# First layer-norm tiles through a ScalarE square root, normalising allowed on Pool, and a new queue order

## Chip, cores and metric

One core of one Trainium2 chip. The metric is device time in microseconds (us) of one execution, as the median of several runs. Profiles are of one execution each; times inside them count from the start of its span. Pool is GpSimd.

## The reference

A pre-layer-norm attention (16 heads, 8 positions at a dilation of 2) and an MLP with two more layer norms, on 2048 rows of 448 values in bf16. Cut to what matters here, the layer norms:

```python
def _layernorm(x, axis=-1, eps=1e-5):
    m = jnp.mean(x, axis=axis, keepdims=True)
    v = jnp.var(x, axis=axis, keepdims=True)
    return (x - m) / jnp.sqrt(v + eps)

x = A_x
h  = x + attention(_layernorm(x), A_wqkv, A_wo)
# B(y): y1 = y + gelu(_layernorm(y) @ w1) shifted @ w2 ; y1 + gelu(_layernorm(y1) @ w3) @ w4
h2 = h + B(_layernorm(h), B_w1, B_w2, B_w3, B_w4)
```

## The kernel before

The 2048 rows are four chunks of four tiles (128 rows each). Every layer norm of a tile is: statistics on VectorE (`bn_stats`, `bn_aggr`), inverse deviation and negative mean times it on Pool (`inv_std`), and one *normalising* of 512 or 448 elements per partition, then a transpose, on TensorE or by a transposing DMA issued from SyncE's queue. There are 64 normalisings. Tags: `A1` is the layer norm before the projections (V, QK), `B1` the one before `W1`, `X` the one kept for the residual, `L3` the one before `W3`.

```python
def inv_std(slot, kind, i0, n, s1=1.0, s2=EPS, with_nmr=True):
    pool("tensor_scalar", 200, out=vtmp[...], in0=mv[..., 1], scalar1=s1, scalar2=s2, op0=ALU.mult, op1=ALU.add)
    pool("tensor_tensor", 420 + 160 * n, out=rstd[...], in0=vtmp[...], in1=mhalf[:, 0:n], op=ALU.pow)
    ...                                            # nmr = -mean * rstd, for ScalarE's form

def normalize(slot, kind, i, out_ap, in_ap, dve_only=False):
    kv = dict(out=out_ap, in0=in_ap, scalar1=m_, scalar2=r_, op0=ALU.subtract, op1=ALU.mult)
    if dve_only:
        return dve("tensor_scalar", 390, **kv)
    op = S.add_many("flex", ...)                   # the queue order decides the engine
    op.opts = {"dve": [("tensor_scalar", kv)],
               "act": [("activation", dict(out=out_ap, in_=in_ap, func=ACT.Identity, scale=r_, bias=n_))]}
    op.occ = {"dve": 308, "act": 652}; op.lat = {"dve": 390, "act": 745}
    return op

def phase_A1(c):
    for il in range(4):
        ln_stats(0, xin[:, i, :], i)
        if c == 0 and il % 2 == 1:
            inv_std(0, 0, i - 1, 2, with_nmr=False)
    ...
    for il in range(4):
        normalize(0, 0, 4 * c + il, ..., dve_only=c == 0)
        transpose_pe(...) if c in TPE else transpose_dma(...)
```

A table `_ORDER` lists every operation once, by number. It gives each engine its queue (each runs in order), the PSUM banks, and, by a suffix `v`, `a` or `p`, the engine of a flexible operation (VectorE, ScalarE, Pool). Waits are derived from it.

Of the kernel before, what the change touches and what calls it, by code (L numbers as in the profile page):

```python
# [5 lines left out]
ACT = mybir.ActivationFunctionType  # L6
# [222 lines left out]
WARM = 18  # L229
LATE = 2  # L230

START = 158


_ORDER = """
2 1 3 4 7 8 5 6 14 12 13 0 16 15 63 62 71 17:7 76 9 10 127 20 18 21 19 26 24 22 23 27 25 28 29 30 33 34:7 31:6
36 32a 37:5 39 40:4 35v 38v 41v 72 44a 45v 47v 108 46a 11 61 102 66 106 75 105 94 100 101 109 48:60 49 50 82:42
83 84 53a 78 69 42 43a 97 110 85 56 98 129 107 135 104 133 67 131 136 130 132 134 137 138 86a 139 140 51 177 178
179 54v 59 60 87a 52:7 181 175 64 55a 180 95 57 217:24 150v 182 70 73 141v 88:60 89 176 90 91 144v 65 68 218 220
93a 151:3 183 145:2 58 147v 146a 142:5 148:4 92v 184 152v 143v 149v 74 99 198 185 186 193v 221 77 219 231:06 232  # L240
234 163:24 164 153 233 165 167a 222:76 191a 189v 103 235 166 168a 227 113p 194 228 229 114p 118p 112p 115a 117a
111p 116a 119p 196 187a 162 169:20 170 171 172 223 224 225 190 343:64 173a 96 195 174a 200 236:32 226 158:1 241
344 242 237 197 346 202 199 161a 375:2 378a 238 154:64 357:02 358 203 188 243 201 239 244 240 204 230 206 345
192 155 120p 360 205 359 361 156 159a 207 157 160a 212a 347 245:02 246 208a 247 248 249 250 251 253 257 255 254
258 252 256 259 386:46 268 387 388 270 389 214a 390a 261 362:32 391a 363 260 367 210a 368 262 269 122 121 364
271 369 379 265a 380:40 209 365 348:76 349 353 381 382 350 351 354 383 384a 385a 532:26 370 352 371:40 372 373
535 79 533 355 376a 374 216 525:26 377a 266v 211 263v 264v 267 366 81 356 526 215 528 272a 536 413:40 414 415
534 537:6 527 529 213 530:2 417 419 126 421 416 275a 418 420 538a 423 425 422 426 424 427 274v 429 428 430 531a
540 438 539 541 542 432v 273a 433v 431v 434v 276:64 277 278 436 437 279 435 280 401:02 402 403 404 281 288v 286a
292v 290v 289a 283v 287v 285v 282v 293v 291v 284v 392:46 439 406a 441v 405a 543 546 442v 393 394 545 544 395  # L250
397a 398a 400 294:02 295 296 298 297 299 302 300 303 301 306 304 305 307 309v 308v 310 125 440a 128 444:46 445
446 447 407:20 408 409 448 449 451v 460v 410 453v 456v 454a 458a 452a 457a 455v 461a 450v 459v 663:64 412a 411v
666 664 547 550 549 548 462:20 463 464 465 466 467 470 396:5 468 474 469 472 473 471 475 399a 313:26 314 315
551:04 316 80 317 552 553 555 554 556 557 559 561 558 562 123 478 476 477 479 124 563 564 560 480v 565 482v 483v
318 481a 486 574 667 567 319:62 320 321 322 324 325:04 326 327 328 566 568 323 331:62 311 312 572v 332 333 334
484 329 330 569v 571v 570v 576 665 335 573 336 670:04 337:7 443a 671 340:6 575 673 674 338 672 341 668:4 577
675:0 676v 487 580a 578a 489:62 669a 490 491 581v 485 493 678 677 582:04 583 584 586 585 587 492 679 680 681 683
684 682 488 494 598v 495:06 496 497 498 592v 599v 588v 596v 590v 594v 591v 589a 593a 595v 597v 600:24 601 602
604 603 606 607 605 608 612 610 613 609 611 614 500 615 616 617 499 501:06 502 686 503 688 505 504 507:42 508
509 685 506 511 687 510 619a 621v 339 513:7 618v 579a 626 689:40 690 514 512 620a 691 693 695 692 697 698 694  # L260
696 701 699 702 700 712 519:7 522:6 705 622 624 520 703 704 523 706 707a 521 623 633:04 634 635 636 710v 515
709v 637 708v 711 639:62 640 641 638 643 625 642 627:40 644 628 629 720:26 630 713 631 714 721 722 723 632 725
715 724 718v 645:04 730v 731 736v 732v 738v 729v 740v 737v 733a 734 728v 735a 727a 726v 739 646 647 649 719a 648
516:7 650 716v 342 517 717v 809:02 810 811 813 812 814 817 815 816 746:64 818 819 820 821 822 747 748 749 751
756 757 750 758 524 754 759 657:3 654:5 651:7 755 752 753 760 762 761 763 658 824v 660:6 823v 825 764a 741 742
743 652 659 744:7 655 766v 767v 765a 771 770 745 653 828:42 829 830 768 661 834:60 831 835 836 837 832 833
840:24 841 838 839 842 843 844 785:06 786 845 846:42 847 848 849 851 827 656 826 769 850 772 787 788 790 789
773:42 774 775 776 777 778 779:06 780 518 791:24 792 793 795 794 781 782 783 662 784 852:3 853 796 854 797:7
803:6 798 799 804 805 806:7 807 800:6 808 801 802 855:7 856 857
""".split()  # L270


def _fast_path(nc, es, flag, A_x, A_wqkv, A_wo, B_w1, B_w2, B_w3, B_w4, out):
# [15 lines left out]
    def sb(name, shape, dt):  # L289
        return es.enter_context(nc.sbuf_tensor(name, shape, dt))  # L290
# [38 lines left out]
    nmr = sb("nmr", [128, 4, NTL], F32)  # L329
    vtmp = sb("vtmp", [128, 4, NTL], F32)  # L330
    mhalf = sb("mhalf", [128, 4], F32)
    fint = sb("fint", [128, 32], I32)
    fmax = sb("fmax", [128, 1], F32)
    fbit = sb("fbit", [128, 1], BF16)
# [6 lines left out]
    def tag(name):  # L341
        S.tag = name
# [4 lines left out]
        return S.add_many("pe", calls, cost, cost + 166, mode=mode)  # L347

    def act(out_ap, in_ap, func, n, **kw):
        table = {ACT.Exp: "exp", ACT.Gelu_apprx_tanh: "gelu"}.get(func)  # L350
        lat = 186 + n / 1.2 + 93 * sum(isinstance(v, bass.AP) for v in kw.values())
        return S.add_many("act", [("activation", dict(out=out_ap, in_=in_ap, func=func, **kw))], lat - 93, lat, table=table)

# [3 lines left out]
    def dve(meth, lat, **kw):  # L357
        return S.add_many("dve", [(meth, kw)], lat - 82, lat)
# [103 lines left out]
    for c in range(1, NCH):  # L462
# [5 lines left out]
    S.add("pool", "affine_select", 300, out=ident[:], in_=ident[:], pattern=[[-1, 128]],  # L468
          compare_op=ALU.not_equal, fill=1.0, base=0, channel_multiplier=1)
    dve("memset", 62, ap=mhalf[:], constant=-0.5)  # L470
    dve("memset", 272, ap=wqk_p[:, :, :, 28:32], constant=0.0)
    pool("memset", 100, ap=hT[:, 0, :, :, 8:16], constant=0.0)
    tag("warm")
# [77 lines left out]
    def inv_std(slot, kind, i0, n, s1=1.0, s2=EPS, with_nmr=True):  # L551
        pool("tensor_scalar", 200, out=vtmp[:, slot, i0:i0 + n], in0=mv[:, kind, i0:i0 + n, 1], scalar1=s1,
             scalar2=s2, op0=ALU.mult, op1=ALU.add)
        pool("tensor_tensor", 420 + 160 * n, out=rstd[:, slot, i0:i0 + n], in0=vtmp[:, slot, i0:i0 + n],
             in1=mhalf[:, 0:n], op=ALU.pow)
        if with_nmr:
            pool("tensor_scalar", 230, out=nmr[:, slot, i0:i0 + n], in0=mv[:, kind, i0:i0 + n, 0], scalar1=-1.0,
                 scalar2=None, op0=ALU.mult)
            pool("tensor_tensor", 220, out=nmr[:, slot, i0:i0 + n], in0=nmr[:, slot, i0:i0 + n],
                 in1=rstd[:, slot, i0:i0 + n], op=ALU.mult)  # L560

    def normalize(slot, kind, i, out_ap, in_ap, dve_only=False):
        r_ = rstd[:, slot, i:i + 1]
        n_ = nmr[:, slot, i:i + 1]
        m_ = mv[:, kind, i, 0:1]
        kv = dict(out=out_ap, in0=in_ap, scalar1=m_, scalar2=r_, op0=ALU.subtract, op1=ALU.mult)
        if dve_only:
            return dve("tensor_scalar", 390, **kv)
        op = S.add_many("flex", [("tensor_scalar", dict(kv, x=n_))], 0, 0)
        op.opts = {"dve": [("tensor_scalar", kv)],  # L570
                   "act": [("activation", dict(out=out_ap, in_=in_ap, func=ACT.Identity, scale=r_, bias=n_))]}
        op.occ = {"dve": 308, "act": 652}; op.lat = {"dve": 390, "act": 745}
        return op

    def lslot():
# [35 lines left out]
    def phase_A1(c):  # L611
        tag("A1_%d" % c)
        s = ls = c % 2
        for il in range(4):
            i = 4 * c + il
            ln_stats(0, xin[:, i, :], i)
            if c == 0 and il % 2 == 1:
                inv_std(0, 0, i - 1, 2, with_nmr=False)
        if c > 0:
            inv_std(0, 0, 4 * c, 4)  # L620
        for il in range(4):
            normalize(0, 0, 4 * c + il, lntm[:, ls, il, :, :], windows(xin[:, 4 * c + il, :]), dve_only=c == 0)
            if c in TPE:
                transpose_pe(ls, il, s)
            else:
                transpose_dma("%d_%d" % (c, il), columns(s, il), lntm[:, ls, il, :, :].rearrange("p a k -> p (a k)"), 1)
        if c > 0:
            tag("Vc_%d" % c)
            pool("tensor_copy", 215, out=hT[:, s, :, :, 8:16], in_=hT[:, 1 - s, :, :, 264:272])
# [311 lines left out]
                   op0=ALU.mult)  # L941

    phase_A1(0)
    pad_wqk()
    phase_V(0)
    init1()
# [535 lines left out]
```

## Time and profile before

| | before |
|---|---|
| median of runs (first three) | 193.94 us |
| span of the profiled run | 192.9 us |
| TensorE busy | 183.2 us (95%) |
| VectorE / ScalarE / Pool busy | 129.7 / 108.6 / 44.2 us |
| one normalising on VectorE / ScalarE | 0.41 / 0.81 us |

TensorE is the bound: what isn't its busy time is 9.7 us. Its waits, stages and opening are shown in the prediction.

### The profile page before, as it was taken

How to read it: one execution, taken by the hardware profiler on the slowest of the kernel's cores; microseconds unless marked ns; L12 is line 12 of the kernel's file. 1: busy time of each engine (PE TensorE's matmuls, PEld its weight loads, DVE VectorE, ACT ScalarE, POOL GpSimd, SP SyncE). 2: the span in 40 equal slices, each digit the busy share in tenths (PEclk: the TensorE clock that was granted, in tenths of full speed). 3: DMA queues.
4: the chain of work that ended last, by engine and by line, in shares of the span. 5: the costliest groups of instructions: out<-in, count | busy, mean ns of one | idle time of the engine just before them, and what ended most of it. 6: DMA issues, size and time to landing. Idle time of an engine off the chain costs nothing.

```text
span 192.9 us, 6787 instructions
## 1 busy us (share of the span) xinstructions
PE 183.2 (95%) x3003; PEld 103.4 (54%) x3003; DVE 129.7 (67%) x312; ACT 108.6 (56%) x140; POOL 44.2 (23%) x107
## 2 busy tenths in 40 slices
PE   7899999999988998999989999999999999999994
PEld 2445645545665764567555454444764557554551
DVE  6899999999997966989773596970079871001221
ACT  2367789757997759859587555045670026554000
POOL 2538750407002402032900023070002300000000
PEclk9999999999999999999999999999999999999999
DMA  5997135411099492920552800427000055000111
GB/s 147 337 294 180 45 58 131 141 31 31 3 159 117 107 227 60 262 102 3 109 115 63 192 3 0 109 65 142 0 3 0 0 135 154 3 0 8 46 51 51
DMA packets 32479, 17.77 MB, mean 92 GB/s; under 512 B 22524, under 2 KB 31932, under 8 KB 32444
## 3 DMA queue, kind: packets, MB, share of 16 engines
q1 hardware_dynamic: 32156, 17.05, 37.6%
q8 instruction: 25, 0.41, 0.9%
q10 hardware_dynamic: 288, 0.23, 0.3%
q14 instruction: 10, 0.08, 0.1%
HBM read 10.07 MB, written 1.90 MB: 62 GB/s over the span
## 4 chain that ended last, share of the span: by engine, by line
PE 72%; DVE 16%; ACT 4%; POOL 3%; issue 1%; DMA 1%
PE ps L1390 72%; DVE st L1390 4%; DVE pt L1390 2%; DVE lntm L1390 2%; DMA xin<-in_A_x_dram 1%; POOL rstd L1390 1%; DVE qk L1390 1%; ACT arena L1390 1%; POOL nmr L1390 1%; DVE xb L1390 1%; DVE xin L1390 1%; DVE osb L1390 1%; ACT qk L1390 1%; ACT pt L1390 1%; ACT vt L1390 1%
## 5 line engine op out<-in xcount | busy, mean ns | idle before, releaser
L1390 PE MATMUL ps<-actT,w_s 64*128 64x512 bf16 (+2 forms) x560 | 44.4, 312 | 0.0
L1390 PE MATMUL ps<-w_s,arena 128*128 128x448 bf16 x224 | 43.4, 353 | 0.4 <-ACT arena L1390 0.4
L1390 DVE TENSOR_TENSOR xb<-ps,xb 128x448 bf16<-128x448 f32 (+1 forms) x26 | 18.5, 725 | 33.7 <-PE ps L1390 33.7
L1390 ACT ACTIVATE arena<-ps 128x512 bf16<-128x512 f32 (+2 forms) x40 | 28.9, 766 | 17.4 <-PE ps L1390 17.4
L1390 PEld LDWEIGHTS ps<-actT,w_s 64*128 64x128 bf16 x560 | 25.9, 94 | 17.1 <-issue 0.4
L1390 PEld LDWEIGHTS ps<-w_s,arena 128*128 128x128 bf16 x224 | 21.4, 98 | 21.5 <-issue 1.0
L1390 PE MATMUL ps<-hT,arena 64*128 64x512 bf16 x224 | 25.8, 377 | 0.0
L1390 POOL TENSOR_SCALAR vtmp<-mv 128x4 f32<-128x4 f32 (+1 forms) x18 | 4.6, 256 | 83.6 <-DVE mv L1390 83.0
L1390 POOL TENSOR_TENSOR rstd<-vtmp,mhalf 128x4 f32<-128x4 f32 (+1 forms) x18 | 18.7, 1041 | 0.8
L1390 DVE BATCH_NORM_STATS2 st<-xin 128x6 f32<-128x448 bf16 x32 | 18.3, 610 | 0.9 <-DMA xin<-in_A_x_dram 0.8
L1390 PEld LDWEIGHTS ps<-hT,arena 64*128 64x128 bf16 x224 | 11.9, 94 | 10.7 <-issue 0.4
L1390 ACT ACTIVATE qk<-ps 128x1024 bf16<-128x1024 f32 x14 | 13.8, 1021 | 5.4 <-PE ps L1390 5.2
L1390 ACT ACTIVATE pt<-ps 128x1024 bf16<-128x1024 f32 x16 | 15.5, 1025 | 2.0 <-PE ps L1390 1.9
L1390 PE MATMUL ps<-arena,hT 64*64 64x448 bf16 (+1 forms) x248 | 15.3, 353 | 0.5 <-DVE hT L1390 0.3
L1390 PE MATMUL ps<-actT,w_p 64*128 64x512 bf16 (+1 forms) x140 | 13.2, 334 | 0.6 <-issue 0.6
L1390 PE MATMUL ps<-wo_s,oT 64*128 64x448 bf16 x128 | 13.1, 350 | 0.6 <-ACT vt L1390 0.6
L1390 DVE COPY gC<-gtm 32x256 bf16<-32x256 bf16 (+1 forms) x23 | 5.1, 223 | 12.5 <-ACT gtm L1390 11.9
L1390 ACT ACTIVATE lntm<-xb,nmr,rstd 128x512 bf16<-128x512 bf16 x5 | 3.9, 807 | 14.8 <-POOL nmr L1390 14.8
L1390 ACT ACTIVATE lntm<-xin,nmr,rstd 128x512 bf16<-128x512 bf16 x8 | 6.3, 818 | 8.8 <-POOL nmr L1390 8.8
L1390 PEld LDWEIGHTS ps<-actT,w_p 64*128 64x128 bf16 x140 | 8.3, 94 | 5.2 <-issue 1.0
L1390 DVE TENSOR_SCALAR lntm<-xin,mv,rstd 128x512 bf16<-128x512 bf16 x24 | 9.6, 444 | 2.2 <-POOL nmr L1390 1.4
L1390 DVE TENSOR_TENSOR pt<-pt,msk 128x1024 bf16<-128x1024 bf16 x16 | 10.9, 713 | 0.2 <-ACT pt L1390 0.2
(84 smaller groups left out, 220.8 us busy)
## 6 DMA issues: line engine op xcount, KB each, us to landing
w_s<-in_B_w_dram SPq DMA_DIRECT2D x6, 448.0 KB, 6.0
rzb<-rz_scratch SPq DMA_DIRECT2D x8, 256.0 KB, 4.6
out_dram<-xb SPq DMA_DIRECT2D x16, 112.0 KB, 1.9
xin<-in_A_x_dram SPq DMA_DIRECT2D x3, 448.0 KB, 7.7
arena<-in_A_wqkv_dram SPq DMA_DIRECT2D x2, 448.0 KB, 6.2
w_s<-in_B_w_dram SPq DMA_DIRECT2D x2, 336.0 KB, 7.5
arena<-in_A_wqkv_dram SPq DMA_DIRECT2D x2, 224.0 KB, 4.6
w_s<-in_B_w_dram SPq DMA_DIRECT2D x2, 224.0 KB, 4.6
```

Of the source, the lines that this page charges most:

```text
L1390: inst = getattr(eng, meth)(**kw)
```

## The change

Three intents: shorten the opening by taking the first inverse deviations off Pool; let Pool, 23% busy, take normalisings from VectorE and ScalarE; lay all queues out anew for that.

```diff
+    def inv_std_first(i0):                        # chunk 0, two tiles at a time
+        act(v, m_[:, :, 1], ACT.Sqrt, 2, bias=epsb[:])
+        dve("reciprocal", 160, out=r_, in_=v)
+        dve("scalar_tensor_tensor", 160, out=n_, in0=m_[:, :, 0], scalar=-1.0, in1=r_, op0=ALU.mult, op1=ALU.mult)
...
-                   "act": [("activation", dict(..., func=ACT.Identity, scale=r_, bias=n_))]}
-        op.occ = {"dve": 308, "act": 652}; op.lat = {"dve": 390, "act": 745}
+                   "act": [("activation", dict(..., func=ACT.Identity, scale=r_, bias=n_))],
+                   "pool": [("tensor_scalar", kv)]}
+        op.occ = {"dve": 308, "act": 652, "pool": 730}; op.lat = {"dve": 390, "act": 745, "pool": 750}
...
-                inv_std(0, 0, i - 1, 2, with_nmr=False)
+                inv_std_first(i - 1)
-            normalize(0, 0, 4 * c + il, ..., dve_only=c == 0)
+            normalize(0, 0, 4 * c + il, ...)
...
+    tag("exp")
+    act(expd[:], epsb[:], ACT.Exp, 1)             # dummy exp; stands last in ScalarE's queue
...
-START = 158
+START = 150
-_ORDER = """ 2 1 3 4 7 8 5 6 14 12 13 0 ...        (all of the table replaced)
+_ORDER = """ 3 14 1 2 12 0 15 17 13 4 7 8 ...
```

In the new table 24 normalisings carry `p`, and 49 other operations after the opening (weight copies, V, QK and probability work) change engine too. The change itself puts 730 and 750 ns on a Pool normalising.

## The prediction

> **What bounds the kernel now.** I read the page first, then the waits of TensorE, then the chain that ended last, then busy time by stage, and last the spread of single durations.
>
> ```profile
> span 192.9 us, 6787 instructions
> PE 183.2 (95%) x3003; PEld 103.4 (54%) x3003; DVE 129.7 (67%) x312; ACT 108.6 (56%) x140; POOL 44.2 (23%) x107
> ```
>
> TensorE is busy for 183.2 of 192.9 us, so all idle time of TensorE together is 9.7 us. The waits of TensorE name where it sits:
>
> ```profile
> PE ps L1390 <- DVE oT L1390: 1.4, 1, 1.4
> PE ps L1390 <- DVE qk L1390: 1.1, 1, 1.1
> PE ps L1390 <- issue: 0.9, 2, 0.6
> PE ps L1390 <- DVE lntm L1390: 0.6, 1, 0.6
> ```
>
> The first is the start: TensorE has nothing before 1.35 us. The last matmul ends at 190.05 and the final VectorE add and store take the other 2.9 us. Neither is touched, so what better ordering could win is 9.7 - 1.4 - 2.9 = 5.4 us, or 2.8%, and only if every wait went. That is the cap on a gain. By stage:
>
> ```profile
> core 0: us, PE busy (x) PEld busy (x) DVE busy (x) ACT busy (x) POOL busy (x), PEclk, DMA share, GB/s
> 9.00:32.00 23.00, 22.37 (x600) 12.28 (x600) 22.16 (x49) 18.01 (x24) 12.24 (x32) 1.00 0.57 148
> 32.00:60.00 28.00, 26.50 (x817) 14.87 (x813) 27.13 (x57) 22.39 (x28) 6.30 (x17) 1.00 0.47 74
> 60.00:78.00 18.00, 16.44 (x281) 11.16 (x283) 13.08 (x40) 13.41 (x19) 4.98 (x14) 1.00 0.62 138
> ...
> 98.00:190.00 92.00, 91.63 (x878) 49.59 (x866) 42.26 (x108) 37.96 (x50) 9.24 (x20) 1.00 0.22 54
> ```
>
> To 60 us VectorE is as full as TensorE (22.16 of 23, 27.13 of 28): there the two engines bound the time together. From 98 us on TensorE has 0.4 us of idle in 92: nothing is to be won there. The opening runs through VectorE and Pool:
>
> ```profile
> 3.50 1.16 DVE st L1390 x2
> ...
> 6.22 0.27 POOL vtmp L1390
> 6.49 0.07 issue
> 6.56 0.76 POOL rstd L1390
> 7.32 0.03 issue
> 7.34 0.99 DVE lntm L1390 x2
> 8.33 0.68 DVE hT L1390 x2
> 9.01 0.04 issue
> 9.05 10.23 PE ps L1390 x194
> ```
>
> The first projection matmul can't start before the fourth transposed tile is copied, at 9.05 us. Of that path, the inverse deviation on Pool takes 1.2 us (6.14 to 7.34).
>
> **What the Trainium skill says, and whether the trace agrees.**
> 1. "SBUF — State Buffer", the section on the two separate sides: VectorE and GpSimd share one port pair as an exclusive lock, and the loser blocks for the whole instruction. VectorE needs it in its 2-port modes or with two inputs in SBUF. The trace agrees, and strongly:
>
> ```profile
> L1390 DVE TENSOR_SCALAR lntm<-xin,mv,rstd x24: 379/407/1123, 6.0 to 128.3; 128x512 bf16<-128x512 bf16 x24
> L1390 DVE TENSOR_TENSOR pt<-pt,msk x16: 648/688/1091, 22.6 to 96.8; 128x1024 bf16<-128x1024 bf16 x16
> L1390 POOL TENSOR_SCALAR nmr<-mv x16: 220/227/1789, 15.6 to 152.5; 128x4 f32<-128x4 f32 x14, 128x2 f32<-128x2 f32 x2
> ```
>
> Columns are minimum, median and maximum in ns. The normalising of 1123 ns began at 24.9 us, while Pool was copying w_p from 22.3 to 26.1; the 1789 ns one on Pool, normally 227, began at 90.7, when VectorE ran normalisings and adds back to back.
> 2. "ScalarE: Activation LUTs", What ACT_TABLE_LOAD costs: a load is about 1283 ns. The trace has six at a mean of 1283 ns. The same page's table-set section puts sqrt and exp in different sets.
> 3. "GPSIMD Engine Reference", section 4.1, advises VectorE for elementwise work and says that one-input operations run roughly at line rate on GpSimd. The trace has no normalising on Pool. It has copies: 1072 ns for 512 and 1494 ns for 1024 elements, thus 422 ns per 512 elements, and 256 ns for a tiny TENSOR_SCALAR. My estimate for a normalising of 512 elements is 256 + 422, about 0.7 us, and up to 1.1 us as the copy.
>
> **The change part by part.**
> (a) *The first inverse deviation.* Removed on Pool: two times (0.2 + 0.73) us. Added: two square roots on ScalarE (estimate 0.28 us each from the fixed cost of its small instructions: 0.25 us for 64 elements, plus a pointer operand), two reciprocals and two products on VectorE (0.16 us each, estimate from the 0.17 us of an aggregate and the 0.24 us of a reciprocal of 16). One of four normalisings (0.82 us) goes to ScalarE, which was idle, and ScalarE now copies two of the four transposed tiles. VectorE from 3.50: statistics and aggregates 2.64 (3.50 to 6.14 in the chain, unchanged), + 4 x 0.16, + 3 normalisings at 0.35, + one copy in the shadow and one exposed (0.35 and 0.4), + about 0.1 of waiting for the transpose: 3.50 + 2.64 + 0.64 + 1.05 + 0.75 + 0.1 = 8.7. Before: 9.05. The gain is 0.3 to 0.4, not 1.2 us, because the four small VectorE instructions stand in a queue that was already full. A part of it is that the 0.67 us normalising at 7.34, which ran beside Pool's mask select, is 0.35 again, as Pool's first selects now come later.
> (b) *The tables.* With sqrt first, exp has to be loaded before the first softmax. The dummy exp that should load it early stands last in the queue order, where it costs nothing and does nothing for the softmax. So 1.28 us enters ScalarE's queue between the last V copy and the first exp. Before, that copy ended at 16.6 and exp began at 16.85, on the end of the scores matmul. After, ScalarE also has one more V copy (0.92). I get copy 16.4, load to 17.7, exp at 17.7 instead of 16.85: 0.9 us late. TensorE has other matmuls to run (the second QK group, about 3.2 us), so I put about half, 0.4 us, on its path, before the second scores.
> (c) *Normalising on Pool.* 24 of 64 go to Pool: 16 from VectorE (42 to 26), 8 from ScalarE (22 to 14). In the first 60 us VectorE loses about 5, 5 x 0.4 = 2 us in the stage where it is a bound; ScalarE loses six, but gets weight packing and V copies instead. Against it stands the lock: about 8 Pool normalisings of 0.7 us fall in that stage, and if half of them meet a VectorE instruction that needs the pair and block it for half their length, that is 8 x 0.5 x 0.35 = 1.4 us. Net: 0 to -1 us on VectorE.
> (d) *The order.* Nearly every queue is permuted, with the same 226 matmul groups. Walking the new TensorE queue with durations from the trace, I find scores of the second chunk done about when they were, the second output projection 0.6 us later (VectorE delivers oT and the V copy late), the first W2 level, and the stage before 86 us about 0.5 us ahead. I hold that walk to about 1 us.
>
> Sum: (a) -0.4, (b) +0.4, (c) -0.5, (d) 0 to -0.5; together about -0.5 us on 193.94: **193.4 us**.
>
> **The rivals.**
> *R1: the order pays.* The waits at 48 to 62 us and at 77 us (0.5 + 0.6 + 0.6 + 1.1 us) are all VectorE lateness or issue. If relief of VectorE removes most of them, the gain is 2 to 2.5 us: 191.5. For it: VectorE is the releaser in most of them. Against: the lock hands back part of the relief, and one of them is issue, which no engine causes.
> *R2: the lock takes over.* If Pool normalisings last 1 us and VectorE queues behind most of them, VectorE loses 24 x 0.5 us, of which the 60 to 98 us stage can hide a part; +1.5 to +3 us: 195.5 to 197. For it: the 1123 and 1789 ns cases. Against: from 98 us VectorE is under half busy and its delays vanish.
> *R3: the exp table is exposed whole,* the delay runs through the masks (VectorE) and the first attention: +0.9 instead of +0.4, 193.9.
>
> **Range and chances.** The cap on a gain is 5.4 us and 2% is 3.9 us: a gain of over 2% needs nearly three quarters of all removable waits to go, with no new ones. I give it 0.03. A loss of over 2% needs R2 at its worst: 0.04. Else within 2%: 0.93. The range is my walk's error of 1 us with the two rivals' milder halves: 191.9 to 195.2.
>
> **What would show it.** (a) right if the first projection matmul starts at 8.6 to 8.8 us; wrong if at 9.0 or later. (b) right if a 1.28 us table load stands right before the first exp, which starts at about 17.7, and TensorE has a gap of 0.3 to 0.7 us between 19 and 24 us. (c) right if VectorE's busy time falls by only 4 to 6 us (16 x 0.4, less the stretched ones), Pool's normalisings have a median of 0.7 to 0.8 us and some of over 1 us, and a few VectorE ones pass 0.6 us. (d) right if TensorE's busy time is 183 us within 1 and its idle time 9 to 10 us. The prediction fails if a new wait of over 1 us on a Pool normalising or its transposing transfer stands in TensorE's waits, or if the waits between 48 and 78 us are gone.

## The result, and the profile after

Ratios here and below are the mean time of one kernel's fast runs over that of the other's fast runs of the same rounds, so not quite the ratio of the medians quoted beside them. A run counts as slow when it took over 1.5% more than the fastest of its kernel, else as fast.

| | before | after |
|---|---|---|
| median (lowest to highest) of 4 runs | 194.34 us (193.91 to 195.06) | 207.21 us (206.53 to 207.99) |
| ratio, 95% interval | | 1.066 (1.060 to 1.072) |
| TensorE busy / idle in the span | 183.2 / 9.7 us | 187.6 / 17.2 us |

The changed kernel is 12.9 us slower; the prediction was 193.4. (Granted clock, 0.975 to 0.983 of full speed, is a mean over the run; what lowers it is shown below.) From the head of the changed kernel's page:

```profile
span 204.8 us, 6799 instructions
...
PE 187.6 (92%) x3003; PEld 103.8 (51%) x3003; DVE 126.0 (62%) x299; ACT 108.5 (53%) x141; POOL 89.2 (44%) x125
```

Pool's busy time has doubled, by 45 us, while VectorE was relieved of only 3.7. Single durations of the normalisings of the changed kernel (minimum/median/maximum in ns), first Pool's two tiles, then VectorE's:

```profile
L1403 POOL TENSOR_SCALAR lntm<-xin,mv,rstd x11: 2070/2086/4021, 16.6 to 105.1; 128x512 bf16<-128x512 bf16 x11
L1403 POOL TENSOR_SCALAR xb<-xin,mv,rstd x9: 1862/1868/2017, 68.0 to 161.1; 128x448 bf16<-128x448 bf16 x9
L1403 DVE TENSOR_SCALAR lntm<-xin,mv,rstd x14: 315/407/415, 6.1 to 142.7; 128x512 bf16<-128x512 bf16 x14
```

The same instruction takes five times as long on Pool. The minimum is as long as the median, so this is its own length; only the maxima are stretched by something else. (The last four of the 24, into `lntm` from `xb`, took 2.07 to 3.16 us.) Waits of TensorE in the changed kernel (engine and tile waited for; us in total, times, longest):

```profile
PE ps L1403 <- DMA actT<-lntm: 4.7, 1, 4.7
PE ps L1403 <- ACT osb L1403: 2.5, 1, 2.5
PE ps L1403 <- DVE mv L1403: 2.0, 1, 2.0
PE ps L1403 <- DVE epsb L1403: 1.4, 1, 1.4
PE ps L1403 <- DVE qk L1403: 1.1, 1, 1.1
```

The last two stood in the kernel before too. The first three, 9.2 us, are new. The chains below show Pool behind the first two; for the third it is argued. (`W1` uses `actT`; `osb` is the attention's output before its division, `mv` a tile's mean and variance.) The chain that ended last, for the first (start us, us, what):

```profile
43.49 1.03 POOL rstd L1403
44.52 0.86 POOL nmr L1403 x2
...
45.76 2.09 POOL lntm L1403
...
48.59 1.05 POOL rstd L1403
...
50.46 6.54 POOL lntm L1403 x3
...
58.89 3.71 DMA actT<-lntm
62.60 0.14 issue
```

Before, `W1` of the first chunk began at 58.43 us. Now Pool runs four normalisings of 2.09 us or more between 45.76 and 57.00, the transposing transfer goes out at 58.89, and TensorE starts at 62.74. The same chain at the second wait:

```profile
101.12 6.07 POOL lntm L1403 x2
107.19 1.02 POOL rstd L1403
...
108.51 0.76 ACT xb L1403
109.27 1.83 ACT osb L1403 x2
111.10 0.05 issue
```

The waits name a ScalarE copy to `osb`, but ScalarE had itself waited for Pool's `rstd`, which stood in Pool's queue behind two normalisings of another chunk. One of the two was stretched, beside VectorE's work of the same time:

```profile
101.10 4.02 POOL L1403 TENSOR_SCALAR lntm<-xin,mv,rstd 128x512 bf16<-128x512 bf16 x1
101.27 1.89 DVE L1403 TENSOR_TENSOR pt<-pt,msk 128x1024 bf16<-128x1024 bf16 x3
```

It took 1.9 us longer than its neighbour (2.08 us). That fits the lock which the prediction names, though no run isolates it, and up to 1.9 of the 2.5 us of this wait may be its doing. The third wait ended at 91.54 us. The transfer of its operand went out at 88.73, right after two Pool normalisings (83.49 to 88.71), and took 2.7 us to land, to about 91.4; the VectorE instruction that is named ended at 91.52. Either can have been the last. For Pool speaks that at this place 0.6 us or nothing is left in two kernels below (three on Pool, and short instructions).

Beside the waits, TensorE's clock fell. Busy time by stretch of the changed kernel (after the length of the stretch: TensorE, its weight loads, VectorE, ScalarE, Pool, then PEclk, the granted clock):

```profile
60.50:67.00 6.50, 4.26 (x26) 2.30 (x28) 1.43 (x6) 0.00 (x0) 3.15 (x5) 0.50 0.70 163
67.50:111.50 44.00, 38.23 (x744) 23.97 (x742) 29.90 (x66) 25.52 (x35) 30.60 (x31) 1.00 0.44 109
112.00:115.00 3.00, 3.00 (x22) 1.63 (x20) 1.37 (x4) 2.33 (x3) 0.29 (x1) 0.50 0.10 22
115.50:204.50 89.00, 85.90 (x776) 46.36 (x772) 38.74 (x97) 36.87 (x51) 17.91 (x25) 1.00 0.21 55
```

The clock was 1.00 in these stages before. Here it was halved twice; slices of 0.5 us put the edges at 60.4 and 67.2, and at 111.6 and 115.0 us. TensorE was busy for 4.5 and 3.4 us of that, so by estimate half speed cost 4.0 of its 4.4 us of extra busy time. 7.5 us more idle and 4.4 us more busy make the span's 11.9. The Trainium skill, "TensorE: Matmul & The Clock Gate", Part 1, says that the clock halves after about one idle window of 3.4 us. The half agrees, and the lengths, 6.8 and 3.4 us, are two and one such window. The idle time fits less well: the first drop came 2.4 us into the wait of 4.7, and the second 0.5 us after the end of a wait of only 2.5.

### The profile page after: what moved, and what is told of

It is laid out like the page before. It is cut to its first block, busy times and chain, and to the rows that moved or that the text cites. A ratio compares the mean times of both kernels' runs of the same rounds, so it can differ in the third digit from the quotient of the medians.

```text
span 204.8 us, 6799 instructions
## 1 busy us (share of the span) xinstructions
PE 187.6 (92%) x3003; PEld 103.8 (51%) x3003; DVE 126.0 (62%) x299; ACT 108.5 (53%) x141; POOL 89.2 (44%) x125
## 4 chain that ended last, share of the span: by engine, by line
PE 61%; POOL 15%; DVE 12%; issue 4%; ACT 4%; DMA 2%; SPq 0%; DVEq 0%; POOLq 0%
PE ps L1403 61%; POOL lntm L1403 7%; POOL rstd L1403 3%; DVE st L1403 3%; POOL nmr L1403 2%; DVE xb L1403 2%; DVE xin L1403 2%; DMA actT<-lntm 2%; DVE gC L1403 2%; DVE oT L1403 1%; POOL xb L1403 1%; POOL vtmp L1403 1%; ACT osb L1403 1%; ACT gtm L1403 1%; DVE gB L1403 1%
## 5 line engine op out<-in xcount | busy, mean ns | idle before, releaser
L1403 POOL TENSOR_SCALAR vtmp<-mv 128x4 f32<-128x4 f32 (+1 forms) x16 | 3.9, 243 | 53.4 <-DVE mv L1403 52.7
L1403 POOL TENSOR_SCALAR lntm<-xin,mv,rstd 128x512 bf16<-128x512 bf16 x11 | 25.2, 2298 | 3.0 <-DMA hT<-lntm 2.7
L1403 PE MATMUL ps<-hT,arena 64*128 64x512 bf16 x224 | 26.5, 377 | 0.0
L1403 PE MATMUL ps<-actT,w_p 64*128 64x512 bf16 (+1 forms) x140 | 17.0, 402 | 7.1 <-DMA actT<-lntm 4.7
L1403 POOL TENSOR_SCALAR xb<-xin,mv,rstd 128x448 bf16<-128x448 bf16 x9 | 17.0, 1891 | 0.4
L1403 PEld LDWEIGHTS ps<-actT,w_p 64*128 64x128 bf16 x140 | 9.6, 109 | 13.9 <-issue 7.5
L1403 PEld LDWEIGHTS ps<-hT,arena 64*128 64x128 bf16 x224 | 10.4, 94 | 11.7 <-issue 0.8
L1403 POOL TENSOR_TENSOR rstd<-vtmp,mhalf 128x4 f32<-128x4 f32 (+1 forms) x16 | 16.0, 997 | 0.8
L1403 ACT ACTIVATE qk<-ps 128x1024 bf16<-128x1024 f32 x13 | 12.9, 1023 | 4.4 <-PE ps L1403 4.2
L1403 ACT ACTIVATE lntm<-xb,nmr,rstd 128x512 bf16<-128x512 bf16 x4 | 3.1, 809 | 16.3 <-POOL nmr L1403 16.3
```

What stands on the lines that cost most here:

```text
L1403: inst = getattr(eng, meth)(**kw)
```

## The experiments

Theory P: the loss comes from what a normalising costs on Pool. Theory Q: it comes from the new order, the other engine moves, or the opening. A point is one per cent of the time before.

### All 24 normalisings off Pool

```diff
- ... 151p ... 197p ... 193p ... 216p ... 270p ... 268p 269p ...   (24 entries of the changed order)
+ ... 151v ... 197v ... 193v ... 216a ... 270v ... 268v 269a ...   (engines of the kernel before)
```

> The changed kernel with one thing undone: its 24 normalisings on Pool go back to the engine that the kernel before gave each (15 VectorE, 9 ScalarE); opening, exp table and queue order stay as changed. Theory P (the loss comes from normalisings that last 2.09 us on Pool instead of 0.4 on VectorE or 0.8 on ScalarE): 193.5 to 195.5 us, the 4.7 us wait of TensorE on the transposing transfer gone, TensorE busy time back from 187.6 to 183 to 184 us. Theory Q (the new queue order or the opening with its exp table loses the time): it stays above 203 us with the long waits still there.

Measured: 198.11 us median, ratio 1.018 (1.013 to 1.022). The profile is of the one slow run (200.93), so its waits aren't read. 4.8 of the 6.6 points go with the engine of the normalisings, 9.4 us; 3.4 us stay, more than theory P allowed. (The edit moves 14 to VectorE and 10 to ScalarE; the 15 and 9 in the expectation are a miscount.)

### The same 24 on Pool in the kernel before

```diff
+                   "pool": [("tensor_scalar", kv)]}           (in the kernel before)
- ... 147v ... 193v ... 189v ... 212a ...
+ ... 147p ... 193p ... 189p ... 212p ...                       (the same 24, old numbers)
```

> The kernel before, in its own queue order and with its own opening, with only the same 24 normalisings moved to Pool. Theory P: clearly slower, 199 to 209 us, with new waits of over 1 us on Pool's normalisings or on the transposing transfers behind them, Pool's busy time near 89 us. Theory Q: 193.5 to 196 us, as the engine of the normalisings would not be what costs.

Measured: 207.3 us, 1.067 (1.060 to 1.074). One part of the change alone costs all that the change costs. The long waits of TensorE are only in part the same: 3.3 us on a Pool copy to `qk`, 2.6 us put down to issue, 2.5 us on `osb`; Pool was busy for 95.4 us. The opening and the new order aren't needed for it.

### The opening alone

```diff
  (changed code; the changed order as far as the last transposed copy of chunk 0, then the old order; START = 158)
```

> The kernel before with only the opening of the change: square root on ScalarE, reciprocal and product on VectorE, one of the four normalisings and two transposed copies on ScalarE, the dummy exp last; the rest in the old order with no normalising on Pool. My reading that the opening and the table together cost nothing (the warm-up matmuls, not the deviation, set when the transposes start): 193.9 to 194.9 us, first projection matmul at 8.9 to 9.1 us, table load of 1.28 us before the first exp with no TensorE wait over 0.3 us. The prediction's own sum (opening -0.4, table +0.4) gives the same time, but the first projection matmul at 8.6 to 8.8 us and a wait of 0.3 to 0.7 us near 19 to 24 us. Rival (the exp table is exposed in the first attention): 195 to 196 us.

Measured: 194.44 us, 1.001 (0.996 to 1.006), the first projection matmul at 8.89 us. The table load hides: ScalarE in the changed kernel, around the first exp:

```profile
15.18 1.41 ACT L1403 ACTIVATE vt<-ps 128x896 bf16<-128x896 f32 x2 [0.33 <-PE ps L1403]
16.61 1.28 ACT L1403 ACT_TABLE_LOAD   x1
17.91 1.94 ACT L1403 ACTIVATE pt<-ps 128x1024 bf16<-128x1024 f32 x2
```

It stands where I said and delays exp to 17.91, but TensorE has other matmuls and shows no wait of over 0.2 us there.

### Fewer warm-up matmuls with that opening

```diff
-WARM = 18
+WARM = 15
```

> The kernel before with the opening of the change alone, as e3_opening_alone, and 15 warm-up matmuls instead of 18. There the last of 18 warm-up matmuls ended at 7.44 us, after the first normalised tile was ready at about 6.5, and the first projection matmul came at 8.89. If the warm-up sets when the transposes start, they start by 6.6 to 6.8 us and the first projection matmul is at 8.3 to 8.6 us, with 0 to 0.4 us off the time: 193.8 to 194.4 us (0.998 to 1.001 of before). If it is VectorE's queue that sets it, the first projection matmul stays at 8.8 to 8.9 us and only an idle gap opens ahead of the transposes.

TensorE's opening with 15 (the first line is the warm-up, the second the transposes, the third the projection):

```profile
1.36 5.39 PE L1401 MATMUL ps<-oT 128*128 128x512 bf16 x15 [1.36 <-DVE epsb L1401]
6.59 1.40 PE L1401 MATMUL ps<-ident,lntm 128*128 128x128 bf16 x16
8.44 1.90 PE L1401 MATMUL ps<-arena,hT 64*64 64x448 bf16 x36 [0.45 <-DVE ones L1401]
```

And in the changed kernel, with 18:

```profile
1.35 6.24 PE L1403 MATMUL ps<-oT 128*128 128x512 bf16 x18 [1.35 <-DVE epsb L1403]
7.42 1.06 PE L1403 MATMUL ps<-ident,lntm 128*128 128x128 bf16 x16
9.03 1.29 PE L1403 MATMUL ps<-arena,hT 64*64 64x448 bf16 x21 [0.55 <-DVE hT L1403]
```

So the warm-up held the opening: the first normalised tile is ready at 6.52 us in the changed kernel, but 18 matmuls run to 7.59. Without three of them the projection starts 0.45 us earlier than in the run before. The time, 194.13 us, 0.999 (0.995 to 1.002), doesn't show it: later stages take the gain back.

### What a Pool instruction costs by its form

```diff
+    for _ in range(3):                          # on the kernel before, at the end of Pool's queue
+        pool("tensor_copy", out=Y, in_=X)                                            # 512 elements
+        pool("tensor_scalar", out=Y, in0=X, scalar1=2.0, scalar2=None, op0=ALU.mult)
+        pool("tensor_scalar", out=Y, in0=X, scalar1=2.0, scalar2=0.5, op0=ALU.subtract, op1=ALU.mult)
+        ...  # the same with per-partition values: one; two at 512, 128, 256, 1024 elements
```

> The kernel before with 24 probe instructions put at the end of Pool's queue, after all its own work (about 154 us on), three rounds of eight forms on bf16 tiles of 128 partitions: copy of 512 elements; multiply by one constant, 512; subtract and multiply with two constants, 512; multiply by one per-partition value, 512; subtract and multiply with two per-partition values (the form of the normalising) at 512, 128, 256 and 1024 elements. From the 448 and 512 element normalisings of the changed kernel (1.87 and 2.08 us) the two-value form should be 0.4 us + 3.25 ns per element: 0.82, 1.24, 2.08 and 3.7 us. Theory S (each of the two operations passes costs per element): one-operation forms about 1.1 to 1.3 us, near the copy's 1.07, two-operation forms 2.0 us whether constant or per-partition. Rival T (the per-partition operand is what costs): two constants as fast as one, about 1.1 us, and one per-partition value already near 1.6 us or more. Rival U (the lock against VectorE stretches them): durations scatter, and fall well below 2 us when VectorE is idle.

Pool's timeline in the first of the three rounds, in the order of the edit after the copy (start us, us, form):

```profile
157.38 1.50 POOL L1404 TENSOR_SCALAR lntm<-lntm 128x512 bf16<-128x512 bf16 x1
158.96 1.94 POOL L1404 TENSOR_SCALAR lntm<-lntm 128x512 bf16<-128x512 bf16 x1
161.00 1.56 POOL L1404 TENSOR_SCALAR lntm<-lntm,mhalf 128x512 bf16<-128x512 bf16 x1
162.67 2.08 POOL L1404 TENSOR_SCALAR lntm<-lntm,mhalf 128x512 bf16<-128x512 bf16 x1
164.85 0.79 POOL L1404 TENSOR_SCALAR lntm<-lntm,mhalf 128x128 bf16<-128x128 bf16 x1
165.75 1.22 POOL L1404 TENSOR_SCALAR lntm<-lntm,mhalf 128x256 bf16<-128x256 bf16 x1
167.06 3.78 POOL L1404 TENSOR_SCALAR lntm<-lntm,mhalf 128x1024 bf16<-128x1024 bf16 x1
```

And the copy, all three of them (mean ns last but one):

```profile
L1404 POOL COPY lntm<-lntm 128x512 bf16<-128x512 bf16 x3 | 1.8, 609 | 2.2 <-DMA actT<-lntm 2.1
```

One constant 1.50, two constants 1.94, one per-partition value 1.56, two 2.08, a copy 0.61 us. The three rounds agree (copies 609 to 610 ns, the 1024-element form 3778 to 3779) while VectorE worked beside them for 7.5 of 39 us, which rules out theory U. Theory T falls too: the per-partition operand adds only 0.06 to 0.14 us. Theory S is nearest, but its split was off: the second operation costs 0.4 to 0.5 us, and going from a copy to any arithmetic costs 0.9. For the normalising's form, 128 and 512 elements give (2.08 - 0.79) / 384 = 3.4 ns per element and 0.36 us fixed. The kernel's own time (201.3) says nothing, as the probes outlast the rest.

### Three off Pool, and one

```diff
- ... 270p ... 268p 269p ...
+ ... 270v ... 268v 269a ...
```

> The changed kernel with only three of the 24 normalisings taken off Pool: those of the first chunk's second layer norm that stand before the transposing transfer on which TensorE waits 4.7 us. Theory P, with the waits adding up: that wait and the slow clock behind it (TensorE granted 0.66 from 60 to 70 us) go, 6 to 8 us in all, so 199 to 201.5 us; the later waits of 2.0 (VectorE mv) and 2.5 us (ScalarE osb) stay. Rival (the time is lost to the shared port or to total Pool load, not to this one wait): it improves by only 3/24 of the 13 us, 1.6 us, to 205 to 206 us, or the wait moves to the next group.

Measured: 202.83 us, 1.041 (1.035 to 1.047), 2.5 points or 4.9 us better. The 4.7 us wait is gone: `W1` starts at 59.51 us without one, and the clock stays at 1.00 there. But 1.9 us, put down to issue, are left between its matmuls. The direction is theory P's; the size is under its 6 to 8 us. The wait had an odd part: of the last three normalisings before it, the third isn't even an operand of the transfer that TensorE waits for. The next kernel puts back that one alone:

```diff
- ... 214p ...
+ ... 214a ...
```

> The changed kernel with one of the 24 normalisings off Pool: the last tile of the fourth input chunk, on ScalarE as before. It is last of the three that Pool runs from 50.46 to 57.00 us, and its transposing transfer stands ahead of the one that TensorE waits for 4.7 us in SyncE's queue. Theory of the queue: that transfer goes out when Pool's previous normalising ends, near 54.9 instead of 58.9 us, TensorE's wait falls from 4.7 to about 0.7 us or less, and the time by 4 to 5 us to 202.3 to 203.5 us, as much as taking the three others off (202.8). Theory of the amount: 1/24 of 13 us, 206.5 us or more.

Measured: 204.48 us median, but in two groups: one fast run at 200.84 (granted clock 0.999) and three at 204.34 to 204.86 (0.983), which count as slow. So there is no ratio, and its size stays open.

### Only SyncE's queue changed

```diff
- ... 215 ... 271 ...      (transfer of the fourth input chunk's tile first)
+ ... 271 215 ...          (transfer of the first chunk's B1 first; all normalisings stay on Pool)
```

> The changed kernel with all 24 normalisings still on Pool and nothing changed but SyncE's queue: the transposing transfer of the first chunk's second layer norm goes ahead of that of the last tile of the fourth input chunk, instead of behind it. Theory of the queue (the first one's operands are ready near 54.9 us, it is held 4 us by its neighbour, which waits for the third of Pool's normalisings): issue near 55 instead of 58.9 us, TensorE's wait for it falls from 4.7 to about 0.7 us or less; 203 to 204 us if the granted clock still falls as in the changed kernel, near 201 if it doesn't. Theory of Pool's own lateness (it is not the neighbour but Pool): wait and time unchanged, 207 us.

Measured: 204.44 us, 1.048 (1.043 to 1.053), 1.8 points or 3.6 us from one entry moved. Two of its six runs count as slow, at a clock (0.975) that the changed kernel's fast runs have too; with them it is 1.5 points. SyncE's queue in the profiled run (a slow one, so only the order of events is read, not the time):

```profile
56.32 1.61 SPq L1401 DMA_TRANSPOSE actT<-lntm  x1
58.31 2.14 SPq L1401 DMA_TRANSPOSE hT<-lntm  x1
```

In the changed kernel the order was the reverse:

```profile
57.03 1.82 SPq L1403 DMA_TRANSPOSE hT<-lntm  x1
58.89 1.66 SPq L1403 DMA_TRANSPOSE actT<-lntm  x1
```

The transfer that matters had been held behind one that waited for Pool's next normalising: its own last operand from Pool was ready at 54.60 us. So part of the first wait was a second in-order queue passing Pool's lateness on. The wait didn't fall to 0.7, though: 3.1 us were left. The kernel with three back, below, shows the same in a fast run (2.8 us left): Pool's second normalising took 3.10 us there instead of 2.07, and the transfer, out at 56.62, took 5.0 us to land instead of 3.7. Why the transfer took longer isn't shown.

### The second wait

```diff
- ... 574p ... 575p ...
+ ... 574v ... 575v ...
```

> The changed kernel with the two normalisings off Pool that run at 101.1 to 107.2 us (third chunk, second layer norm), back on VectorE as before. Theory P: the wait of 2.5 us on ScalarE osb at 108.7 us, which follows Pool's rstd and nmr behind these two, goes, and with it the lowered clock from 98 to 130 us: 2.5 to 3.5 us, so 203.7 to 204.7 us; the 4.7 and 2.0 us waits stay. Rival (the wait has another cause, as ScalarE's queue is named): no change, 207 us.

Measured: 203.3 us, 1.044 (1.039 to 1.049), 2.2 points or 4.3 us better. The 2.5 us wait on `osb` is gone, the 4.7 and 2.0 stay: it was Pool's, though ScalarE is named.

### Three back, and their counterpart

```diff
  214a, 574v, 575v in the changed order, the other 21 on Pool        (first kernel)
  214p, 574p, 575p in the changed order, the other 21 off Pool       (second kernel)
```

> The changed kernel with three of the 24 normalisings off Pool: the last tile of the fourth input chunk (ScalarE) and the pair of the third chunk's second layer norm (VectorE), which single runs showed to be worth 2.7 to 6.4 and 3.9 us. If the waits add up and these three are most of what Pool costs: 198 to 201 us, against 197.7 with all 24 off Pool and 207.2 with none. If the cost is spread over the 24: 206 us.

> The counterpart: the changed kernel with only those three normalisings on Pool and the other 21 back on VectorE and ScalarE. If these three instructions are what costs, wherever the rest runs: 203 to 206 us. If they cost only because Pool's queue is already late with the others before them: 197.5 to 200 us, near the 197.7 of none on Pool.

Measured: 200.9 us, 1.028 (1.023 to 1.033), and 199.97 us, 1.029 (1.024 to 1.034). Three of 24 bring 3.8 of the 4.8 points that all 24 bring. Alone on Pool they cost 1.1 points over none. Both sit between the extremes: the pair at 101 us costs its wait whatever runs before (2.4 us on `osb` is there in the second kernel), while number 214 seems to cost only when Pool's queue is already late: in the second kernel `W1` starts at 60.45 us without a wait before it.

### Where Pool is idle

```diff
- ... 189v ... 212a ...                 (old order)
+ ... 189p ... 212p ...
```

> The kernel before, in its own order, with two normalisings on Pool, picked from stretches where Pool sat idle: one of the third and one of the fourth input chunk, whose results are needed many us later. If a Pool normalising of 2.08 us can pay where Pool is idle and nobody waits: 193.0 to 194.2 us. If even there it holds up Pool's small copies and the shared port: 194.8 to 196.5 us.

Measured: 194.09 us, 0.997 (0.993 to 1.000). Two normalisings in Pool's idle stretches do no harm; a gain isn't established. Both small gains with the new opening:

```diff
  opening of the change, WARM = 15, 193p and 216p (new numbers) in the old order
```

> Candidate for a better kernel: old order, new opening, 15 instead of 18 warm-up matmuls (0.9987 of before), and the two normalisings that Pool could take in its idle stretches (0.9969 of before). If small gains add: 0.995 to 0.997 of before, 193.2 to 194.0 us. If each was only scatter: 0.998 to 1.001.

Measured: 194.39 us, 0.999 (0.997 to 1.001). They were scatter, or don't add. No version here beats the kernel before.

### The 3.4 us left, first try

```diff
  changed order, all 73 moved operations on their old engines          (first kernel)
  old order, new opening, the 49 other moves, no normalising on Pool   (second kernel)
```

> The changed kernel's opening and queue order, but every later instruction that the change moved to another engine (73 in all: the 24 normalisings and 49 others such as weight copies, V, QK and probability work) on the engine of the kernel before. With the 24 alone moved back it was 1.018 of before (197.7 us). If the residue of 3.4 us is the other 49 moves (more copies and normalisings on ScalarE than it can take): 194 to 195.5 us. If it is the queue order itself, arranged around normalisings that are elsewhere: 197 to 200 us.

> The complement: the old queue order with the new opening (which measured 1.001) and the 49 other engine moves of the change, no normalising on Pool. If those moves are the residue: 197 to 198.5 us. If the order is: 193.7 to 195.5 us.

Measured: 206.89 us, 1.065 (1.062 to 1.068), and 202.93 us, 1.043 (1.040 to 1.046). Neither expectation holds. The order without the moves costs 6.5 points, the moves without the order 4.3, both together 1.8. An order and an assignment of engines are one thing: half of either is a kernel that nobody laid out, and such undoing says little about its parts. That applies to the 3.4 us of the first experiment too. So the last pair undoes nothing and only shortens the 24 instructions in place.

### The 24 Pool instructions made short

```diff
-                   "pool": [("tensor_scalar", kv)]}
+                   "pool": [("tensor_copy", dict(out=out_ap, in_=in_ap))]}
```

> The changed kernel with order, engines and opening as they are, but each of Pool's 24 normalisings replaced by a Pool copy of the same tile (wrong values on purpose), which the form probe measured at 0.61 us for 512 elements instead of 2.08. The change's own annotation plans a Pool normalising at 730 ns, close to my 0.7. If the length of these instructions is the whole cause, order included: 192 to 195 us, all of the waits of 4.7, 2.5 and 2.0 us gone. If the order is also bad in itself, by the 3.4 us that were left with the normalisings on VectorE and ScalarE: 196.5 to 198.5 us. If lengths don't matter: 207 us.

> The same replacement in the kernel before with the 24 on Pool, which measured 1.0665 of before with full normalisings. If the length is what cost there: 193 to 195.5 us. If it is that the old order doesn't fit those 24 on Pool whatever they last: 199 us or more.

Their outputs are wrong, which doesn't matter for the times. A copy also has no need of the statistics, but Pool's queue order is kept. Measured: in the changed kernel 196.44 us, 1.007 (1.000 to 1.013), in the kernel before 195.19 us, 1.001 (0.996 to 1.006). With full normalisings in the same places they were 1.066 and 1.067. The busy line of the changed kernel's page with short Pool instructions:

```profile
PE 183.2 (94%) x3003; PEld 103.9 (53%) x3003; DVE 127.1 (65%) x299; ACT 108.8 (56%) x141; POOL 53.7 (28%) x125
```

The durations of its copies into one tile (minimum/median/maximum ns):

```profile
L1403 POOL COPY lntm<-xin x11: 606/612/2569, 16.3 to 96.7; 128x512 bf16<-128x512 bf16 x11
```

TensorE at the place of the first wait, and at that of the second:

```profile
59.27 1.68 PE L1403 MATMUL ps<-actT,w_p 64*128 64x512 bf16 x17
...
102.96 1.26 PE L1403 MATMUL ps<-actT,w_p 64*128 64x512 bf16 x11 [1.01 <-DMA actT<-lntm]
```

TensorE's busy time is back at 183.2, so the clock is restored as well. The first wait is gone, and so is the one on `mv`; 1.0 us is left where 2.5 stood on `osb`. Five short waits put down to issue, 3.2 us in all, are more than the 0.9 us before. Length is the cause of about 6 of the 6.6 points in the new order and of practically all in the old one. The stretching isn't: at the place of the second wait one copy took 2.57 us instead of 0.61, again beside VectorE's three products, and the time came back all the same. The new order itself, with the opening, the other moves and short instructions like those it was laid out for (0.61 us; planned 0.73), costs between 0 and 1.3%.

## Why the prediction was wrong

It said 193.4; measured were 207.2. By its steps:

- **(c), the failed step: the length of a Pool normalising.** I put it at "256 + 422, about 0.7 us, and up to 1.1": the fixed cost of a tiny TENSOR_SCALAR plus the per-element cost of a *copy*. Measured 2.09 for 512 elements and 1.87 for 448. The 1.07 us copy behind it had itself been stretched: the same copy to `w_p` took 0.62 in the probe's kernel. The probe shows the flaw: a copy of 512 takes 0.61 us, the same tile with one operation 1.50, with the normalising's two 2.08. The change's own annotation, 730 ns, has the same size as my mistake, and my walk of its queues therefore found nothing late. 24 x 0.7 would have been 17 us more on Pool; the three tiles took about 52. Replacing length alone restores the time (1.007 and 1.001).
- **The relief of VectorE** was put at 16 x 0.4 us less stretching, 4 to 6; 3.7 came. It bought no time: TensorE now waited for Pool, and even with short Pool instructions the kernel isn't faster (1.007).
- **The lock** was put at 1.4 us on VectorE. The stretched cases fit it (a Pool normalising reached 4.02 us, a VectorE one 0.78), and the 4.02 us stand in the chain of the second wait. It isn't the main cause: Pool's minimum of 2.07 is the length without stretching, and with copies one was still stretched, to 2.57, while the time came back.
- **(d), the order: 0 to -0.5 us.** With short Pool instructions it is 1.007 (1.000 to 1.013), so 0 to +2.5 us. (The four terms add up to -0.5 to -1.0, not to "about -0.5".) Which of its permutations would cost that is open.
- **(a), the opening: -0.4 us.** VectorE's part went as worked out, with tile 0 ready at 6.52 us, but I overlooked that the 18 warm-up matmuls last to 7.59 (7.02 in the profile before). The projection came at 9.03 (before 9.05), where I had 8.7.
- **(b), the tables: +0.4 us.** The load and exp were where I put them (16.61 and 17.91), but nothing was exposed; (a) and (b) together measured 1.001.
- **Rival R2** had the right trigger, Pool normalisings of over 1 us, and the wrong path: I let VectorE queue behind Pool and sized it at 24 x 0.5. VectorE didn't queue: its normalisings into `lntm` from `xin` stayed at 0.41 us, 0.415 at most. TensorE waited for Pool's results, through transfers and ScalarE, and for Pool's `rstd` behind them. The prediction's last sentence named just this sign (a new wait of over 1 us on a Pool normalising's transposing transfer), but the chance of a loss over 2% was put at 0.04.
- **A term that was missing:** the granted clock. TensorE's 4.4 us of extra busy time are over a third of the span's growth. It came back with the waits gone.

What stays open: the size of number 214's share (its runs fell in two clock groups), what ended the wait on `mv`, what part of the second wait is stretching, and whether the new code alignment (`START`) does anything; it wasn't tested alone.

## What to carry to other kernels

An estimate for an operation on another engine needs a duration of that operation on that engine; a copy there is no stand-in for arithmetic, and a probe of eight forms in an idle queue settles it in one run. Before moving work to an idle engine, compare not its share of busy time but its queue ahead of each consumer: here Pool was 23% busy, and four long instructions, passed on by a second in-order queue, made TensorE wait 4.7 us, more than the 3.7 us by which VectorE was relieved. When an order and an engine assignment were made together, undoing half measures the mismatch; change the suspected cost in place instead.

## What the Trainium skill lacked or had wrong

- "GPSIMD Engine Reference", § 4.1, calls one-input elementwise operations roughly line-rate on GpSimd. That doesn't hold here for arithmetic: one operation on 512 bf16 elements took 1.50 to 1.56 us, two 2.08, against 0.41 on VectorE, a factor of 5. It is nearer for a copy, at 0.61.
- The same page, § 3.1, gives one ratio to VectorE, 1.96 for a two-input fp32 add. It lacks TENSOR_SCALAR: about 0.36 us + 3.4 ns per element with two per-partition values, and little less with constants (1.94 against 2.08 us at 512 elements).
- "SBUF — State Buffer", the section on the two separate sides: nothing in the runs speaks against the lock. The page lacks how long a row of VectorE instructions can hold up one Pool instruction: beside three products in a row a normalising took 4.02 us instead of 2.08, and a copy 2.57 instead of 0.61, if it was the lock.
- "TensorE: Matmul & The Clock Gate", Part 1: the clock was halved, as it says, for 6.8 us around a wait of 4.7 us. It was also halved for 3.4 us after a wait of 2.5 us, yet stayed at 1.00 after one of 2.4 us in the kernel with three on Pool. So a gap shorter than the stated idle window can be followed by a halving; how much idling it takes isn't shown.
